# A new order of operations, wider output products and 1 KB weight packets in a DeltaNet and soft-MoE kernel

## The chip, the cores and the metric

The kernel runs on one core of a Trainium2 chip. A core has five engines that work side by side: TensorE (PE in the profile, with its weight loads as PEld), VectorE (DVE), ScalarE (ACT), GpSimd (POOL) and SyncE (SP, which here only issues DMAs). Data moves between main memory and the on-chip memory SBUF by 16 DMA engines; TensorE writes its results to PSUM, a small memory of eight banks, from which VectorE or ScalarE copies them out. DMAs are issued by SP, ACT and POOL. The metric is the time of one execution in microseconds; the median of several executions is compared.

## The reference

All data are float32. The first block is a DeltaNet recurrence over 768 positions, for 4 batches of 8 heads of width 48:

```
state = 0
for t in range(768):
    kt, vt, bt = k_n[:, :, t], v[:, :, t], beta[:, :, t]      # k_n: k over its norm
    y[t]  = q[t] . state
    state = state + bt * outer(kt, vt - state . kt)
```

Its output, as 3072 tokens of width 384, goes into a soft mixture of 8 experts with 4 slots each (32 slots):

```
logits     = x @ phi                           # 3072 x 32
slot_input = softmax(logits, over tokens).T @ x
for each expert e:                             # w1: 384 x 1024, w2: 1024 x 384
    slot_out[e] = relu(slot_input[e] @ w1[e]) @ w2[e]
out        = softmax(logits, over slots) @ slot_out
```

The experts' weights are 12.6 MB each for w1 and w2, 25.2 MB together, and are read once.

## The kernel before

**The recurrence.** It is worked in 12 chunks (called steps, n) of 64 positions, for all 32 pairs of batch and head at once, two chunks to a group g. Loads of k and v (L410) come as five DMAs for each half of the partitions, loads of q (L421) as one. For each chunk the kernel transposes k and q on TensorE (L473), forms their inner products (L504) and copies them out under masks on ACT and DVE. For each group it inverts a triangular matrix (`invert`, from L550): a chain of 15 columns, each a multiplication and a subtraction that the helper at L277 issues on DVE or on POOL, then `join` (from L641) with products on TensorE (L716, L761). Then `step` (from L803) multiplies the state with k (L821), the joined inverse with the rest (L840) together with the late part of the previous chunk's output (L782), updates the state (L867) and multiplies it with q (L791). `route` (from L894, transposes at L902) and `pair` (from L910; logits at L920, transposes at L945, L962 and L982, slot sums at L953) bring each finished group into the soft mixture.

**The experts.** The tokens' maxima are merged and the slot inputs formed (L1054 to L1069). `first` multiplies them with w1 in two batches of four experts (L1090, 24 matmuls for each half of the 1024 columns), clamps (L1099) and transposes (L1106). The second layer is worked in two halves of 192 output columns (h): 128 matmuls with w2 (L1123), a sum over experts (ACT at L1128, TensorE at L1129, DVE at L1130), and then the output products (`comb`, L1142) of the mixing weights with the slots. Each `comb` writes two PSUM banks with eight matmuls, one copy (through the helper at L281 on ACT or L283 on DVE) brings 768 columns to SBUF, and two puts with two DMAs each (L1150) write them out in runs of 768 B. In each half h there are six of these: three groups of tokens (g2) by two halves of rows (z).

**The order.** The code first describes 1164 operations with what they read and write, and then issues them in the sequence that a list written out in the file gives (ORDER, a list of the operations' numbers). Two further lists choose for each operation one of the engines it may run on (ALTS) and for each buffer its address in SBUF or its PSUM bank (PLACE). Semaphores between the engines follow from what each operation reads and writes; on one engine the instructions run in the list's sequence. The list was made ahead of time and the file holds only its result. The weights' loads (L1029 for w1, two DMAs of 256 KB for each of 24 tiles; L1040 for w2, two of 192 KB for each of 32 tiles) are operations of this list like all others, on SP or POOL, and each waits until the last work on its buffer's earlier contents is done.

Of the kernel before, what the change touches and what calls it, by code (L numbers as in the profile page):

```python
# [11 lines left out]
ALU = mybir.AluOpType  # L12
# [184 lines left out]
def kernel(  # L197
# [823 lines left out]
    for e in range(E):  # L1021
        for kk in range(NKT):
# [3 lines left out]
            def go(q, e=e, kk=kk, t=t):  # L1026
                s = moe_w1[e].rearrange("(p k) f -> p k f", k=NKT)
                for x in H2:
                    ENG[q].dma_start(out=A(t)[:, 512 * x:512 * x + 512], in_=s[:, kk, 512 * x:512 * x + 512])  # L1029
# [152 lines left out]
```

## Time and profile before

| | us |
|---|---|
| median of three runs | 296.75 (294.59 to 299.53) |
| the profiled execution | 296.42 |
| its span, first to last instruction | 294.7 |
| TensorE busy, matmuls | 228.9 (78%) |
| VectorE busy | 197.6 (67%) |
| ScalarE busy | 145.2 (49%) |
| GpSimd busy | 140.2 (48%) |

The profile is of one execution. Its span is divided into what each engine did; its chain follows the work that ended last back to the start, and names at each step what released it. "Issue" in the chain, or as the reason of a wait, is time in which an engine waited for nothing that the profile shows. A row of a timeline gives the start, the length, the engine and line, what was done, how many instructions were merged into the row, and in brackets how long the engine had been idle before and what ended that. A row of waits gives the engine and line, what it waited for, the total, the number of times and the longest. A row on the instructions of a line gives the least, the median and the greatest duration in ns. A small q behind an engine's name (SPq) marks its sequencer, which issues the DMAs.

By time the trace falls into four parts: the start, up to the first products at 7.9 us; the recurrence, with the mixture's logits inside it, up to about 248 us; the two expert layers, L1090 from 249.6 and L1123 from 262.5; and the output, whose first DMA is issued at 271.8 us.

### The profile page before, as it was taken

Reading aid. Unit: us, or ns where it says so; the run is one execution under the profiler, and the core shown is the slowest. Engines: PE = TensorE matmul, PEld = TensorE weight load, DVE = VectorE, ACT = ScalarE, POOL = GpSimd, SP = SyncE. Lnnn points to the kernel's source line nnn. Section 1 sums busy time; section 2 is a strip of 40 time slices with the busy share of each in tenths; the row PEclk is TensorE's granted clock in tenths of the full one; section 3 lists DMA queues with packets and bytes.
Section 4 is the critical chain, followed back from the end, with each engine's and each line's share of the span. In section 5 each row is a group of like instructions: output and inputs, shape, how many; then the busy total and the mean of one; then the engine's idle time right before and its main releaser. Section 6 shows DMA issues by size and latency. Waiting matters only on the chain.

```text
span 294.7 us, 14440 instructions
## 1 busy us (share of the span) xinstructions
PE 228.9 (78%) x6252; PEld 186.2 (63%) x6252; DVE 197.6 (67%) x504; ACT 145.2 (49%) x325; POOL 140.2 (48%) x225
## 2 busy tenths in 40 slices
PE   0784778982988897798979877787866988999950
PEld 0663677872887786686868775766654864366640
DVE  3468979989866689777699889883773667213130
ACT  1253487774828466668736768562311532230321
POOL 8997569454493364226762545641640320200460
PEclk9997599999579999999899999999997999999985
DMA  8979642453431361336545407785696599990887
GB/s 147 162 155 166 111 79 56 97 107 56 87 56 34 73 118 33 62 54 136 116 94 118 153 4 232 215 190 177 200 349 218 178 349 375 349 364 13 213 226 206
DMA packets 81519, 45.13 MB, mean 153 GB/s; under 512 B 63520, under 2 KB 74704, under 8 KB 81456
## 3 DMA queue, kind: packets, MB, share of 16 engines
q1 hardware_dynamic: 72704, 30.28, 42.3%
q0 software_dynamic: 5232, 12.56, 15.0%
q10 hardware_dynamic: 3520, 1.38, 2.0%
q8 instruction: 49, 0.80, 1.1%
q14 instruction: 14, 0.11, 0.1%
HBM read 39.47 MB, written 4.72 MB: 150 GB/s over the span
## 4 chain that ended last, share of the span: by engine, by line
PE 27%; DVE 12%; issue 8%; SPq 4%; ACT 4%; POOL 2%; DMA 1%; DVEq 0%; POOLq 0%; ACTq 0%
SPq L1150 4%; DVE sb L277 4%; PE pb L1090 4%; PE pb L716 3%; PE pb L821 3%; ACT sb L281 2%; PE pb L1123 2%; PE pb L782 2%; PE pb L902 2%; PE pb L791 2%; POOL sb L277 2%; PE pb L504 2%; PE pb L867 1%; PE pb L920 1%; PE pb L953 1%
## 5 line engine op out<-in xcount | busy, mean ns | idle before, releaser
L281 ACT ACTIVATE sb<-pb 128x512 f32<-128x512 f32 (+5 forms) x144 | 76.0, 559 | 91.2 <-PE pb L473 22.9
L277 POOL TENSOR_TENSOR sb<-sb 128x256 f32<-128x256 f32 (+10 forms) x89 | 64.7, 735 | 66.8 <-DVE sb L277 33.5
L277 DVE TENSOR_TENSOR sb<-sb 128x126 f32<-128x126 f32 (+10 forms) x153 | 52.9, 347 | 11.2 <-POOL sb L277 6.7
L283 DVE COPY sb<-pb 128x512 f32<-128x512 f32 (+5 forms) x43 | 26.2, 617 | 27.3 <-PE pb L473 5.9
L473 PE MATMUL pb<-sb 128*128 128x128 f32 x192 | 32.7, 318 | 15.0 <-DMA sb<-in_q_dram 9.6
L473 PEld LDWEIGHTS pb<-sb 128*128 128x128 f32 x192 | 24.7, 161 | 19.4 <-issue 11.7
L716 PE MATMUL pb<-sb 64*64 64x32 f32 x1152 | 27.3, 231 | 11.9 <-DVE sb L277 4.7
L716 PEld LDWEIGHTS pb<-sb 64*64 64x64 f32 x1152 | 25.0, 147 | 15.2 <-issue 7.3
L504 PE MATMUL pb<-sb 64*64 64x128 f32 x768 | 28.2, 287 | 5.8 <-ACT sb L281 4.2
L840 PE MATMUL pb<-sb 64*64 64x48 f32 x768 | 26.2, 220 | 3.9 <-DVE sb L770 1.9
L840 PEld LDWEIGHTS pb<-sb 64*64 64x64 f32 x768 | 24.2, 135 | 6.6 <-DVE sb L770 2.5
L504 PEld LDWEIGHTS pb<-sb 64*64 64x64 f32 x768 | 22.7, 140 | 9.0 <-ACT sb L281 5.4
L782 PE MATMUL pb<-sb 64*64 64x48 f32 x768 | 26.0, 220 | 2.3 <-issue 2.3
L782 PEld LDWEIGHTS pb<-sb 64*64 64x64 f32 x768 | 24.1, 135 | 2.7 <-issue 2.5
L1040 POOL DMA_DIRECT2D sb<-in_moe_w_dram x18 | 9.7, 543 | 32.9 <-PE pb L953 16.1
L821 PE MATMUL pb<-sb 128*64 128x96 f32 x352 | 19.2, 260 | 3.2 <-ACT sb L281 1.6
L791 PE MATMUL pb<-sb 128*64 128x96 f32 x352 | 18.9, 261 | 1.9 <-ACT sb L513 0.8
L412 POOL DMA_DIRECT2D sb<-in_k_dram x35 | 19.7, 570 | 0.7 <-DVE sb L341 0.7
L821 PEld LDWEIGHTS pb<-sb 128*64 128x64 f32 x352 | 16.8, 145 | 4.9 <-ACT sb L281 2.2
L1150 POOL DMA_DIRECT2D out_dram<-sb x14 | 8.4, 607 | 23.8 <-DVE sb L283 18.5
L513 ACT ACTIVATE sb<-pb,sb 128x128 f32<-128x128 f32 x48 | 16.9, 368 | 4.9 <-PE pb L504 4.7
L791 PEld LDWEIGHTS pb<-sb 128*64 128x64 f32 x352 | 16.4, 145 | 3.6 <-issue 1.5
(142 smaller groups left out, 376.4 us busy)
## 6 DMA issues: line engine op xcount, KB each, us to landing
sb<-in_moe_w_dram SPq DMA_DIRECT2D x46, 192.0 KB, 5.5
sb<-in_moe_w_dram SPq DMA_DIRECT2D x32, 256.0 KB, 4.0
sb<-in_moe_w_dram POOLq DMA_DIRECT2D x16, 256.0 KB, 5.3
sb<-in_moe_w_dram POOLq DMA_DIRECT2D x18, 192.0 KB, 6.1
sb<-in_q_dram SPq DMA_DIRECT2D x14, 192.0 KB, 4.4
out_dram<-sb SPq DMA_DIRECT2D x24, 96.0 KB, 3.5
sb<-in_v_dram SPq DMA_DIRECT2D x22, 96.0 KB, 3.3
sb<-in_v_dram SPq DMA_DIRECT2D x88, 24.0 KB, 2.8
```

The lines of the kernel that those rows point to most:

```text
L277: ENG[e].tensor_tensor(*a, **kw)
L281: nc.scalar.activation(o, i, ACT.Copy)
L283: V.tensor_copy(o, i)
L412: ENG[e].dma_start(out=d()[p0:p0 + w, x], in_=s[t0:t0 + w, hs])
L473: nc.tensor.transpose(A(ps)[:, 0, P * j:P * j + P], A(src)[:, x:x + P], ident())
L504: mm(A(ps)[ha(r), c, P * j4:P * j4 + P].rearrange("p (a t) -> p a t", a=2), x[ha(c), j, r, 0], x[ha(c), j, r])
L716: mm(A(ps)[ha(b), x, 64 * j:64 * j + RW].rearrange("p (a t) -> p a t", t=w), st, m)
L782: mm(pv(pY)[ha(1 - r), j // 4, j % 4, c], A(at)[ha(r), 512 * c + 64 * j:512 * c + 64 * j + 64], hv(u)[ha(r), j, c], start=first and c == 0 ...
L791: mm(A(pY)[ha(1 - r), j // 4, 96 * (j % 4):96 * (j % 4) + 96], kqv(KQ[n])[:, j, r, 1], Sv(n)[:, j, r], start=j % 4 == 0)
L821: mm(A(pR)[ha(r), j // 4, 96 * (j % 4):96 * (j % 4) + 96], kqv(KQ[n])[:, j, r, 0], Sv(n)[:, j, r])
L840: mm(pv(pW)[ha(r), j // 4, j % 4, c], A(zs)[ha(r), 64 * (zj * c + z0 + j):64 * (zj * c + z0 + j) + 64], hv(R)[ha(r), j, c])
L1150: ENG[e].dma_start(out=o[y, b, z][:, 2 * g2:2 * g2 + 2, HD * h:HD * h + HD], in_=A(ob)[ha(y), Dm * b:Dm * b + Dm].rearrange("p (x d) -> p ...
```

## The change

Three things change.

- All three lists are new. The new order comes from a search under 16 sets of disturbances. By the lists, TensorE's operations keep nearly their old sequence. Of the 24 tiles of w1, 22 are loaded by SP and 2 by POOL, where it was 16 and 8; of the 32 tiles of w2, SP has 23 and POOL 9, as before, though not the same ones. Among the elementwise operations of the recurrence, 12 more of the inversions' multiplications and subtractions run on POOL than before.
- The loads of w1 keep their two DMAs for each tile, but each now gathers two runs of 256 columns (1 KB) for each partition where it had one of 512 (2 KB). The columns then lie in SBUF in another sequence; the clamp puts them back.
- An output product covers both halves of rows (z): 16 matmuls, alternating over the four groups of 32 rows, into four PSUM banks. For two of the three groups of tokens, one of the pairs of banks is the one that holds the state's update during the recurrence (`pS`). The copies and puts are as before, in another sequence and on other engines. The program has 1158 operations.

```
             def go(q, e=e, kk=kk, t=t):
                 s = moe_w1[e].rearrange("(p k) f -> p k f", k=NKT)
                 for x in H2:
-                    ENG[q].dma_start(out=A(t)[:, 512 * x:512 * x + 512], in_=s[:, kk, 512 * x:512 * x + 512])
+                    ENG[q].dma_start(out=A(t)[:, 512 * x:512 * x + 512].rearrange("p (a f) -> p a f", a=2),
+                                     in_=s[:, kk].rearrange("p (a b f) -> p b a f", a=2, b=2)[:, x])
...
             def relu(e, f=f, ph=ph):
-                o = A(hr)[:, f * HF:f * HF + HF]
+                o = A(hr).rearrange("p (a b f) -> p b a f", a=2, b=2)[:, f]
+                i = A(ph)[:, 0].rearrange("p (a f) -> p a f", a=2)
...
         for g2 in range(NG // 2):
-            for z in H2:
-                po, ob = pl.buf(2, psum=True), pl.buf(2 * Dm)
-
-                def comb(po=po, z=z, g2=g2, so=so):
-                    for x in H2:
+            po = [pS if z == g2 % 2 == 0 else pl.buf(2, psum=True) for z in H2]
+            obs = [pl.buf(2 * Dm) for _ in H2]
+
+            def comb(po=po, g2=g2, so=so):
+                for x in H2:
+                    for z in H2:
                         for b in H2:
                             p0 = 32 * (2 * z + b)
                             g = 2 * g2 + x
-                            mm(A(po)[:, b, HD * x:HD * x + HD], A(cT)[p0:p0 + 32, P * g:P * g + P], A(so)[p0:p0 + 32])
-                pl.op("PE", 0.72, comb, r=[(cT, 2 * g2), (cT, 2 * g2 + 1), so], w=[po], rec=8, hold=[ob], act=384)
+                            mm(A(po[z])[:, b, HD * x:HD * x + HD], A(cT)[p0:p0 + 32, P * g:P * g + P], A(so)[p0:p0 + 32])
+            pl.op("PE", 0.8, comb, r=[(cT, 2 * g2), (cT, 2 * g2 + 1), so], w=po, rec=16, hold=obs, act=768)
+            for z in H2:
+                ob = obs[z]
...
```

In the new list all twelve puts of the first half stand ahead of the first output product of the second half, and on ACT three of them stand ahead of the copy at L1128 for that half.

More of the change, by code (lines that the diff above doesn't have):

```diff
@@ new lines @@
+    "0010000000000001010000010000000010001000001111101000110000100110100211210000011022000010000000001000"
+    "0001000000000010000000000001011000001100000000001000010100000001000000000110011001001110000110000001"
+    "0010021201010001100200000000000000000001010001000000001000000000010000101000000000001000010100000001"
+    "0000000000100001010000010100000000000100000001010000000110010001000212010000001000010000100000000000"
+    "0000000000000000010000000000100000000000000000000000101100000110010000000100000010000011010000020011"
@@ L121 @@
+    "1110011111010000000000101010002020101001110020000000000000010000000000000000000010100000000100000000"
+    "0000000100100010000000000000110000000000001000000000000100000010000000000000100100001000000010000010"
+    "0000000000001000000000001000000000001010100001001000000101000000110100000000000000000000000101000000"
+    "0000001010100122121012101000000000000000110000001010121121"
 )
@@ L1094, in relu @@
             def relu(e, f=f, ph=ph):
[L1095 removed]
+                o = A(hr).rearrange("p (a b f) -> p b a f", a=2, b=2)[:, f]
+                i = A(ph)[:, 0].rearrange("p (a f) -> p a f", a=2)
                 if e == "DVE":
[L1097 removed]
+                    V.tensor_scalar(o, i, 0.0, XMSK(qq), op0=ALU.max, op1=ALU.mult)
                 else:
[L1099 removed]
+                    nc.scalar.activation(o, i, ACT.Relu, scale=XMSK(qq))
             pl.op([("ACT", 0.69), ("DVE", 0.75)], None, relu, r=[ph, cxm], w=[(hr, f)])
```

21 lines of the change are left out of this document (5 added, 16 removed), and 172 rows, old and new, of tables (ORDER, PLACE).

## The prediction

> **What bounds the kernel now.** I read the page's shares first, then the chain of work that ended last, then the waits of TensorE, then windows of the DMA traffic, and last the tail's timeline.
>
> ```profile
> span 294.7 us, 14440 instructions
> PE 228.9 (78%) x6252; PEld 186.2 (63%) x6252; DVE 197.6 (67%) x504; ACT 145.2 (49%) x325; POOL 140.2 (48%) x225
> ...
> q8 instruction: 49, 0.80, 1.1%
> ...
> PE 27%; DVE 12%; issue 8%; SPq 4%; ACT 4%; POOL 2%; DMA 1%; DVEq 0%; POOLq 0%; ACTq 0%
> ```
>
> TensorE has the most work, and no engine is full. The chain changes engines all through the recurrence; 8% of the span, some 23 us, is "issue", in which the engine on the chain waits for nothing that the profile shows. The row of queue q8 says what that may be: 49 packets of program code, 0.80 MB, which is 16 KB each. TensorE has 6252 matmuls and 6252 weight loads; 12504 / 49 = 255 instructions, or 64 B of code for each. So TensorE's code streams in through the DMA engines all the time, beside the weights. Its waits between 183 and 225 us:
>
> ```profile
> PE pb L920 <- issue: 4.1, 1, 4.1
> PE pb L782 <- issue: 2.3, 2, 1.2
> PE pb L716 <- issue: 1.9, 2, 1.1
> PE pb L902 <- ACT sb L281: 1.0, 1, 1.0
> PE pb L821 <- issue: 0.8, 1, 0.8
> PE pb L791 <- issue: 0.8, 1, 0.8
> ```
>
> With "issue" that is 9.9 us in seven stalls, each inside a group of matmuls that are alike and need nothing new. The longest cuts one product in two, with the DMA engines full:
>
> ```profile
> 219.01 0.77 PE pb L920 x18
> 219.79 4.13 issue
> 223.92 0.58 PE pb L920 x6
> ```
> ```profile
> 212.00:224.00 12.00, 6.70 (x253) 5.68 (x253) 6.28 (x13) 1.28 (x5) 3.41 (x7) 1.00 0.97 335
> 224.00:240.00 16.00, 15.58 (x406) 12.99 (x410) 10.57 (x30) 5.24 (x15) 3.18 (x6) 0.89 0.64 206
> 240.00:264.00 24.00, 21.85 (x235) 10.68 (x231) 9.56 (x40) 8.77 (x25) 3.20 (x6) 1.00 1.04 368
> ```
>
> The columns are the stretch, the busy time of PE, PEld, DVE, ACT and POOL, TensorE's clock, the share of the DMA engines, and GB/s. At 212 to 224 the DMA engines are 97% busy with weights and TensorE works 6.7 of 12 us; at 240 to 264 they are full again, and TensorE works nearly all the time. So the recurrence's end loses about 10 us to code that comes late, and the two expert layers are bound by TensorE with the weights only just in time. The tail is different:
>
> ```profile
> 271.79 20.12 SPq L1150 DMA_DIRECT2D out_dram<-sb  x24
> ```
> ```profile
> 278.84 13.07 SPq L1150 DMA_DIRECT2D out_dram<-sb  x16
> 282.67 5.78 ACTq L1150 DMA_DIRECT2D out_dram<-sb  x4
> 289.41 1.84 ACTq L1150 DMA_DIRECT2D out_dram<-sb  x2
> ```
> ```profile
> L1150 SPq DMA_DIRECT2D out_dram<-sb x24: 595/626/1495, 271.8 to 291.3; - x24
> L1150 POOL DMA_DIRECT2D out_dram<-sb x14: 602/602/641, 272.9 to 286.8; - x14
> L1150 ACTq DMA_DIRECT2D out_dram<-sb x10: 602/622/780, 272.9 to 290.6; - x10
> ```
>
> SP and ACT issue as if they were one queue: 16 + 6 issues in 13.07 us are 0.594 us each, what one alone takes at best (595 ns). All 34 of the tail fill 271.79 to 291.9: 20.1 / 34 = 0.592. POOL issues beside them. The issue of the output by SP and ACT is the tail's bound, not TensorE.
>
> **The output products.** Each half of the output columns now has three product operations of 16 matmuls in place of six of 8.
>
> ```profile
> 269.84 0.95 PE L1142 MATMUL pb<-sb 32*128 32x192 f32 x16
> ...
> 275.62 0.92 PE L1142 MATMUL pb<-sb 32*128 32x192 f32 x8
> ...
> 279.91 4.35 PE L1142 MATMUL pb<-sb 32*128 32x192 f32 x48 [0.51 <-DVE sb L1130]
> ```
>
> ```profile
> L1142 PE MATMUL pb<-sb 32*128 32x192 f32 x96 | 8.9, 341 | 0.8 <-DVE sb L1130 0.5 <-DVE sb L283 0.2
> ```
>
> Sixteen over all four row groups take 0.95 us (the first row is two old operations of different halves, back to back), 8 alone take 0.92. Six operations of 0.95 are 5.7 us against 8.9 now: 3.2 us less TensorE work, worth nothing where the queue is full. It would be worth up to 3.2 us if copies waited for products. What counts is the split of the 24 copies out, of two DMAs each: the new list gives SP and ACT 15 (30 DMAs) and POOL 9, against 17 (34) and 7. Full from the first to the last, the queue would take 30 x 0.592 = 17.8 us, 2.4 less. I do not expect it full: on ACT the sum of the second layer's last half stands behind three copies out, and the queue runs dry near 278. From there I count 20 issues from 279.0: 279.0 + 20 x 0.594 = 290.9, against 291.9 now. **-1.0 us**, ends -2.4 and +1.2 (if ACT's copies hold the second half's start by two issues more). POOL, with 18 x 0.60 = 10.8 us, has room. Of its section on issuing engines, the Trainium skill (DMA: Bandwidth & Descriptors, "Issuing engines are not separate DMA queues") says that issuing from several engines saves the sequencers' issue time; SP and ACT at 0.594 us together show no such saving here. By that rule the second half's issues would end with SP's twelve alone, about 2.3 us sooner than I count.
>
> **First-layer weights.** The loads keep their bytes but are read in 1 KB runs, two for each partition in place of one of 2 KB.
>
> ```profile
> L1029 SPq DMA_DIRECT2D sb<-in_moe_w_dram x32: 327/382/1363, 133.6 to 250.2; - x32
> L1029 POOL DMA_DIRECT2D sb<-in_moe_w_dram x16: 536/537/603, 160.5 to 236.0; - x16
> ```
> ```profile
> L1040 SPq DMA_DIRECT2D sb<-in_moe_w_dram x46: 327/335/1575, 213.5 to 262.3; - x46
> ```
>
> A plain issue costs SP 0.38 us; the nearest with two runs for each partition is the output's, 0.60. The list puts 44 of these 48 DMAs on SP and 4 on POOL (32 and 16 before): on SP 44 x 0.60 - 32 x 0.38 = +14 us over 110 us, behind which loads of v and of the second layer wait. SP is on the chain for L1150 alone; behind step 10's product it has 14 x 0.60 + 42 x 0.33 = 22 us of issues in 45 us. I take **0**; without that cover the issues on SP cost their own length, 0.2 us a DMA. POOL gets 12 x 0.54 = 6.5 us back. For the transfer itself the nearest rows are the tail's 768 B packets and the stretch at 240:
>
> ```profile
> 271.80:291.90 20.10, 11.90 (x162) 8.92 (x162) 4.98 (x6) 5.18 (x7) 8.43 (x14) 0.84 0.83 221
> ```
>
> 221 / 0.83 = 266 GB/s of a full set of engines, against 368 / 1.04 = 354. A 1 KB packet lies between: 0 to 33% dearer. That matters only where the engines are full; little of the first layer falls there. It goes into the next term.
>
> **The lists.** Both lists hold TensorE's products in nearly the same sequence, so its work does not move. What moves is the weights. Counting from the lists: between step 8's product of the joined inverse (operation 903) and step 10's (951) stand 6.9 MB of weights before, 4.4 MB after, 36% less; behind step 10's stand 14.5 MB before, 16.5 after. In the trace the stretch between these products is roughly 189 to 219 us, that of the stalls.
>
> *Code stalls.* Bounds: 0 (the DMAs may still be issued in a burst as soon as buffers come free) and -9.9. I take them down with the bytes, 36%: **-3.5 us**. The Trainium skill (DMA: Bandwidth & Descriptors, "Queues, rings and completion order") states that an engine goes round its queues by packets of typically 9 to 17 descriptors. By that rule, halved descriptors would halve the wait of code behind first-layer loads, an estimate of -5 us; but a stall of 4.13 us is longer than one such packet of each queue, so the trace bears the rule out only in part.
>
> *The bus.* 2.0 MB more in the last stretch are 2.0 / 0.368 = 5.4 us of full bus. The stretch 224 to 240 has room for (368 - 206) x 16 us = 2.6 MB. Ends 0 and +5.4; I take **+1.0**, near the room, for packets that cost more and room that isn't met.
>
> *VectorE and GpSimd.* Net 16 elementwise operations go from DVE to POOL.
>
> ```profile
> 129.89 0.29 DVE sb L277
> ...
> 130.32 0.43 POOL sb L277
> ```
>
> On the chain each costs 0.14 us more, +2.2 in all; if DVE's queue is what is late, each takes 0.29 off it, -4.6. The chain alternates between both; **0**, with both ends kept.
>
> *The start.* POOL now clears a 1056-column buffer (L558) and a pad ahead of the identity matrix and of its half of k; the first q is split over two queues.
>
> ```profile
> 0.81 1.44 ACTq L421 DMA_DIRECT2D sb<-in_q_dram  x2
> ...
> 5.80 0.97 POOL L558 MEMSET sb<- 128x1056 f32 x1
> ...
> 7.89 1.09 PE L473 MATMUL pb<-sb 128*128 128x128 f32 x4 [7.89 <-DMA sb<-in_q_dram]
> ...
> 10.68 3.53 PE L473 MATMUL pb<-sb 128*128 128x128 f32 x15 [1.30 <-DMA sb<-in_k_dram]
> ```
>
> The first transposes may come sooner, but the second batch waits for k, whose POOL half moves back by up to 0.97 + 0.30 = 1.3 us. Ends -1.3 and +1.3; **+0.5**. The clamp's two-part pattern reads and writes the same elements, and the output's use of the recurrence's PSUM banks waits for work over since step 10: 0 each.
>
> **Sum.** -1.0 - 3.5 + 1.0 + 0.5 = -3.0 on the profiled execution's 296.42 us (span 294.7 and 1.7 around it): 293.4. The median of the runs shown, 296.75, is 0.3 above that execution, so I predict 293.7.
>
> **Rivals.** *The stalls go almost wholly* (8 to 9.9 us of them, with the tail's 1 to 2.4): 285 to 290. For it speaks that nothing else on TensorE is late there by more than 1.0 us; against it, that loads bunch behind step 10 as well, and the full bus at 240 to 264, which would wait for the same bytes. Chance 0.2.
>
> *The bus becomes the bound of the second layer* (the slower side). If buffers come free no sooner than the list places the loads, the 2.0 MB fall behind 240, into a bus that is full, and the second layer waits for its last weights: +5.4, with up to 1.4 for dearer packets (a third of the 4.7 MB of first-layer loads that stand behind step 10's product: 4.2 us x 0.33), no stall removed, the tail's -1.0: 300 to 303, up to 305 if the start's 1.3 and POOL's 2.2 come on top. It decides once less than 2.0 of the 2.6 MB of room is met. Chance 0.25.
>
> *The change does not do what it says*: loads bunch as before, code stalls move elsewhere, the tail gains nothing: 295 to 298. Chance 0.15. The forecast itself, 291 to 296, has 0.4.
>
> **How the numbers follow.** The range, 287 to 303, cuts off the lower part of the first rival and the upper end of the second, about 2 in 10. About 2%, 5.9 us, is what a measurement of this kernel tells from no change (its three runs span 1.7%). Below 290.8 lies the first rival and little else, 0.2; above 302.7 the upper part of the second, 0.16; within, 0.64.
>
> **What would show it.** Right: "issue" waits of TensorE between steps 8 and 11 near 6 us instead of 9.9; no wait of the second layer's products for weights; SP and ACT issues of the output at 0.59 us over about 19 us; L1142 with 16 in 0.95 us throughout. Wrong: weight loads landing behind the second layer's first product, new "issue" stalls after 224 us, or a recurrence whose steps come at other times for reasons of the list that no single row shows; the last is what could most easily upset the sum.

## The result, and the profile after

| | us |
|---|---|
| kernel before, beside the changed kernel | 298.14 (294.59 to 301.26) |
| changed kernel | 307.97 (307.21 to 313.19) |
| changed kernel, once more, in a later set of runs | 306.89 (305.25 to 307.69); before there 297.64 |
| ratio | 1.039, 95% interval 1.027 to 1.050; the second time 1.030, 1.023 to 1.037 |

The change makes the kernel slower by 3 to 4%, 9 to 10 us, where I had forecast 3 us less. The profiled execution of the first set took 313.19 us, 5 us over the median; so the profile shown here is that of the second set (307.69 us, span 306.0), and the first is called "the first profile" where it is used. Ratios leave disturbed executions out, so for a kernel whose executions lie far apart the ratio can be well under that of the medians.

The page's shares, and its clock row (tenths of full speed in 40 slices):

```profile
span 306.0 us, 14470 instructions
PE 229.3 (75%) x6252; PEld 187.0 (61%) x6252; DVE 199.5 (65%) x493; ACT 149.2 (49%) x328; POOL 142.8 (47%) x230
...
PEclk9996699998596999899999979999997799999955
```

TensorE's busy time is that of before (228.9), but only as a sum: its output products take 2.4 us less, and the recurrence and the expert layers, with the same products, 2.8 us more. Most of the 11.3 us more of span is idle time. Windows of both kernels say where; the columns are the stretch, the busy time of PE, PEld, DVE, ACT and POOL, TensorE's granted clock, the DMA engines' share, and GB/s. The stretches end where the last matmul starts of step 0's product, step 3's product, step 7's state update, step 8's product, the merge of the maxima, the last product of the second layer, and the end. Before:

```profile
0.00:52.10 52.10, 33.39 (x634) 28.76 (x636) 37.65 (x122) 24.82 (x59) 41.84 (x75) 0.90 0.73 125
52.10:99.80 47.70, 39.04 (x1245) 34.57 (x1242) 37.13 (x89) 29.55 (x61) 24.12 (x40) 0.89 0.40 73
99.80:177.90 78.10, 67.00 (x2277) 57.98 (x2272) 65.17 (x145) 51.95 (x115) 38.75 (x52) 0.98 0.40 86
177.90:188.80 10.90, 8.22 (x337) 7.26 (x328) 9.46 (x28) 7.17 (x17) 5.09 (x11) 1.00 0.79 224
188.80:249.00 60.20, 46.92 (x1339) 36.87 (x1329) 37.98 (x101) 21.57 (x58) 19.86 (x32) 0.97 0.78 254
249.00:277.70 28.70, 28.27 (x416) 16.12 (x416) 7.04 (x20) 6.39 (x13) 4.59 (x8) 1.00 0.74 241
277.70:294.70 17.00, 6.02 (x66) 4.65 (x58) 3.20 (x4) 3.76 (x6) 5.96 (x10) 0.73 0.80 219
```

After, the second profile:

```profile
0.00:53.90 53.90, 34.54 (x640) 29.34 (x640) 40.22 (x125) 25.79 (x61) 40.79 (x72) 0.91 0.77 125
53.90:104.30 50.40, 40.10 (x1234) 35.48 (x1231) 38.97 (x87) 28.84 (x60) 23.48 (x38) 0.83 0.38 66
104.30:184.20 79.90, 67.23 (x2271) 58.38 (x2271) 62.62 (x137) 52.11 (x114) 37.07 (x53) 0.96 0.41 93
184.20:198.60 14.40, 9.69 (x378) 8.72 (x367) 10.89 (x27) 10.45 (x23) 7.36 (x17) 1.00 0.38 93
198.60:259.40 60.80, 45.74 (x1307) 36.24 (x1298) 33.54 (x91) 23.90 (x58) 22.25 (x31) 0.94 0.85 267
259.40:287.00 27.60, 27.35 (x423) 15.40 (x423) 9.13 (x24) 5.48 (x10) 4.73 (x8) 1.00 0.66 221
287.00:306.00 19.00, 4.62 (x58) 3.39 (x50) 4.16 (x5) 2.65 (x4) 7.17 (x12) 0.63 0.78 208
```

Length less busy time is TensorE's idle time; length times (1 - clock) is what the half clock can have cost there, if TensorE was busy.

| stretch | length, change | idle before, after | (1 - clock) x length before, after |
|---|---|---|---|
| to step 0's product | +1.8 | 18.7, 19.4 | 5.2, 4.9 |
| to step 3's product | +2.7 | 8.7, 10.3 | 5.2, 8.6 |
| to step 7's update | +1.8 | 11.1, 12.7 | 1.6, 3.2 |
| to step 8's product | +3.5 | 2.7, 4.7 | 0, 0 |
| to the merge | +0.6 | 13.3, 15.1 | 1.8, 3.6 |
| both expert layers | -1.1 | 0.4, 0.3 | 0, 0 |
| the tail | +2.0 | 11.0, 14.4 | 4.6, 7.0 |
| sum | +11.3 | 65.9, 76.7 | 18.4, 27.3 |

There is no one hole. Every stretch of the recurrence has 0.7 to 2.0 us more of idle time, the tail 3.4, and there is more half clock. By what ended it, the idle time ahead of the first product with w1 grew in one kind alone in this pair: "issue" from 11.0 to 19.4 us, all the rest together 43.5 and 42.7. Of the 19.4 us, 7.6 lie ahead of the end of step 7's update, where this profile of the kernel before has none; the other seven profiles with its early lists have 1.1 to 4.4 there, so part of that belongs to the execution. Between 183 and 240 us the "issue" waits are much the same, 11.7 us in four lines against 11.0, and TensorE also waits for ScalarE's copies:

```profile
PE pb L840 <- issue: 5.6, 2, 4.2
PE pb L821 <- ACT sb L281: 3.2, 3, 2.3
PE pb L791 <- issue: 2.9, 1, 2.9
PE pb L867 <- issue: 1.9, 2, 1.3
PE pb L791 <- ACT sb L281: 1.5, 1, 1.5
PE pb L716 <- DVE sb L283: 1.5, 2, 0.8
PE pb L821 <- issue: 1.3, 1, 1.3
```

Between step 7's update and step 8's product the timeline shows what the order changed. The new list has ScalarE widen group 4's joined inverse in two instructions (L739) behind the four state copies, and all that the join still has to do comes behind that, up to VectorE's last operation (L770), which releases step 8's product at 196.47. The product of the state with k (L821) waits 2.34 us for the state copies. Step 9's product with q (the second L791) goes ahead of step 8's product, but costs nothing here: it ends at 196.43, L770 at 196.42:

```profile
183.55 0.90 PE L867 MATMUL pb<-sb 64*48 64x48 f32 x64
...
187.24 2.49 ACT L739 ACTIVATE sb<-sb 128x1024 f32<-128x1024 f32 x2
...
187.26 1.54 PE L821 MATMUL pb<-sb 128*64 128x96 f32 x32 [2.34 <-ACT sb L281]
...
190.30 1.54 PE L791 MATMUL pb<-sb 128*64 128x96 f32 x32 [1.50 <-ACT sb L281]
...
194.89 1.54 PE L791 MATMUL pb<-sb 128*64 128x96 f32 x32
...
195.01 1.41 DVE L770 SCALAR_TENSOR_TENSOR sb<-pb,sb 128x512 f32<-128x512 f32 x2 [0.88 <-PE pb L716]
```

Before, one half was on each of ScalarE and VectorE, and both were done ahead of the update, which ended at 178.12, so that a product of the join (L761) ran while the state was copied:

```profile
174.11 1.27 ACT L739 ACTIVATE sb<-sb 128x1024 f32<-128x1024 f32 x1 [0.82 <-DVE sb L733]
...
175.41 0.75 DVE L741 TENSOR_SCALAR sb<-sb 128x1024 f32<-128x1024 f32 x1 [0.23 <-ACT sb L739]
...
177.93 1.57 PE L761 MATMUL pb<-sb 64*64 64x32 f32 x64
...
180.94 1.54 PE L821 MATMUL pb<-sb 128*64 128x96 f32 x32 [1.44 <-ACT sb L281]
```

The state copies are no later than they were: from the update's end to L821 it is 2.8 us in both. From L821 to the start of step 8's product it is 5.6 us before (186.52) and 9.2 us after (196.47); that is where this stretch got longer.

In the tail the timeline of the second profile has ScalarE's sequencer issue six DMAs while its copy of the second half's sum (L1130) waits; TensorE stands for 2.72 us:

```profile
282.26 20.09 SPq L1155 DMA_DIRECT2D out_dram<-sb  x18
...
284.62 4.91 ACTq L1155 DMA_DIRECT2D out_dram<-sb  x6
...
285.77 1.51 PE L1125 MATMUL pb<-sb 128*32 128x192 f32 x32
...
289.63 0.32 ACT L1130 COPY sb<-pb 128x192 f32<-128x192 f32 x1 [7.43 <-DMA out_dram<-sb]
...
290.00 0.59 PE L1131 MATMUL pb<-sb 128*128 128x192 f32 x2 [2.72 <-ACT sb L1130]
...
291.10 3.75 PE L1145 MATMUL pb<-sb 32*128 32x192 f32 x48 [0.51 <-DVE sb L1132]
```

### The profile page after: what moved, and what is told of

It reads as the page before. It is cut to its first block, busy times and chain, and to the rows that moved or that the text cites. A ratio compares the mean times of both kernels' runs of the same rounds, so it can differ in the third digit from the quotient of the medians.

```text
span 311.5 us, 14470 instructions
## 1 busy us (share of the span) xinstructions
PE 240.2 (77%) x6252; PEld 196.2 (63%) x6252; DVE 197.4 (63%) x493; ACT 149.6 (48%) x328; POOL 142.6 (46%) x230
## 4 chain that ended last, share of the span: by engine, by line
PE 49%; DVE 22%; issue 9%; ACT 8%; POOL 4%; DMA 2%; ACTq 2%; SPq 1%; POOLq 0%; DVEq 0%
PE pb L473 7%; PE pb L716 6%; PE pb L840 6%; DVE sb L277 5%; PE pb L504 4%; PE pb L1091 4%; PE pb L791 4%; ACT sb L281 3%; PE pb L821 3%; POOL sb L277 3%; PE pb L1125 3%; PE pb L867 3%; PE pb L902 2%; PE pb L782 2%; PE pb L1145 2%
## 5 line engine op out<-in xcount | busy, mean ns | idle before, releaser
L281 ACT ACTIVATE sb<-pb 128x512 f32<-128x512 f32 (+4 forms) x141 | 76.0, 570 | 83.6 <-PE pb L473 24.9
L277 POOL TENSOR_TENSOR sb<-sb 128x256 f32<-128x256 f32 (+8 forms) x104 | 71.9, 701 | 96.2 <-DVE sb L277 40.0
L277 DVE TENSOR_TENSOR sb<-sb 128x96 f32<-128x96 f32 (+10 forms) x140 | 46.6, 335 | 12.4 <-POOL sb L277 8.6
L283 DVE COPY sb<-pb 128x128 f32<-128x128 f32 (+5 forms) x46 | 25.9, 580 | 33.6 <-PE pb L867 8.7
L473 PE MATMUL pb<-sb 128*128 128x128 f32 x192 | 35.0, 334 | 13.6 <-DMA sb<-in_q_dram 5.3
L716 PE MATMUL pb<-sb 64*64 64x32 f32 x1152 | 29.3, 236 | 13.8 <-DVE sb L277 4.2
L716 PEld LDWEIGHTS pb<-sb 64*64 64x64 f32 x1152 | 26.9, 153 | 17.6 <-issue 8.5
L473 PEld LDWEIGHTS pb<-sb 128*128 128x128 f32 x192 | 26.7, 172 | 17.7 <-issue 8.2
L840 PE MATMUL pb<-sb 64*64 64x48 f32 x768 | 30.5, 238 | 8.5 <-DVE sb L770 4.2
L840 PEld LDWEIGHTS pb<-sb 64*64 64x64 f32 x768 | 28.2, 154 | 11.4 <-DVE sb L770 5.1
L782 PE MATMUL pb<-sb 64*64 64x48 f32 x768 | 29.1, 231 | 0.5 <-issue 0.5
L504 PEld LDWEIGHTS pb<-sb 64*64 64x64 f32 x768 | 24.6, 149 | 6.5 <-ACT sb L281 4.4
L782 PEld LDWEIGHTS pb<-sb 64*64 64x64 f32 x768 | 26.8, 146 | 0.8 <-issue 0.7
L791 PE MATMUL pb<-sb 128*64 128x96 f32 x352 | 19.6, 264 | 4.7 <-issue 3.0
L821 PE MATMUL pb<-sb 128*64 128x96 f32 x352 | 18.3, 252 | 6.4 <-ACT sb L281 3.5
L1155 POOL DMA_DIRECT2D out_dram<-sb x18 | 10.8, 607 | 24.7 <-DVE sb L283 19.9
L821 PEld LDWEIGHTS pb<-sb 128*64 128x64 f32 x352 | 16.0, 140 | 8.2 <-ACT sb L281 5.5
L791 PEld LDWEIGHTS pb<-sb 128*64 128x64 f32 x352 | 16.9, 147 | 6.5 <-issue 3.8
```

The source lines that it names most:

```text
L277: ENG[e].tensor_tensor(*a, **kw)
L281: nc.scalar.activation(o, i, ACT.Copy)
L283: V.tensor_copy(o, i)
L473: nc.tensor.transpose(A(ps)[:, 0, P * j:P * j + P], A(src)[:, x:x + P], ident())
L504: mm(A(ps)[ha(r), c, P * j4:P * j4 + P].rearrange("p (a t) -> p a t", a=2), x[ha(c), j, r, 0], x[ha(c), j, r])
L716: mm(A(ps)[ha(b), x, 64 * j:64 * j + RW].rearrange("p (a t) -> p a t", t=w), st, m)
```

## The experiments

They are told in the order in which they were run. "Old" and "new" are the lists of the kernel before and of the changed one. The kernel before ran beside them with a median of 298.96 in the first set, then 297.78, 298.26, 297.64 and 297.64.

### Which of the three parts

**The packets.** In the changed kernel the loads of w1 and the clamp are put back; in the kernel before they alone are changed.

```
-  ENG[q].dma_start(out=A(t)[:, 512 * x:512 * x + 512].rearrange("p (a f) -> p a f", a=2),
-                   in_=s[:, kk].rearrange("p (a b f) -> p b a f", a=2, b=2)[:, x])
+  ENG[q].dma_start(out=A(t)[:, 512 * x:512 * x + 512], in_=s[:, kk, 512 * x:512 * x + 512])
```

> The changed kernel with the first layer's weights in runs of 2 KB again and the clamp as it was; the lists and the wide output products stay. The time to be explained is some 10 us (298 to 308). Theory A (the new lists make the recurrence and the tail late, packets do nothing): 306 to 309, the same as the changed kernel, and TensorE's issue stalls between steps 8 and 11 stay near 9 to 10 us. Rival B (1 KB runs slow the loads, and with them the code that TensorE waits for): 299 to 302, with those stalls shorter.

> The kernel before with the first layer's weights in runs of 1 KB and the clamp to match; its lists and its output products stay. Theory A: within 1% of before (295 to 301), SP's issue of a first-layer load 0.6 us in place of 0.38, issue stalls of TensorE between 183 and 225 us still near 10 us. Rival B: 303 to 308.

Changed kernel with 2 KB runs: 312.2 (303.85 to 318.26), above both ranges and too scattered to tell the theories apart. Kernel before with 1 KB runs: 299.07, ratio 1.0017 (0.9974 to 1.0060), with 9.7 us of "issue" between 183 and 240 us against 11.0 in the kernel before. So with the old lists the packets cost nothing and gain nothing that can be told; rival B is out there.

**The tail.** Old lists up to the second layer's first product, then the new ones, with the new output products and 1 KB runs (the edit is to the three lists alone). And in the changed kernel, three puts of the first half go from ScalarE to SyncE:

```
   # ALTS, operations 1114, 1115, 1117 (put)
-  ACT
+  SP
```

> The old order, engines and addresses up to the second layer's first product; from there on the new ones with the wide output products (five tail buffers at other addresses); 1 KB runs throughout. Theory A: the tail alone costs 2 to 4 us, 299 to 302, and the second layer's first product starts within 2 us of before's 262.5. If the tail were all of it: 307. If the tail cost nothing (rival C): 297 to 299.

> The changed kernel with three copies out of the first output half issued by SP in place of ACT, those that stand ahead of the copy that starts the second half. Theory A: the second half's sum starts as soon as TensorE has its products, about 2.5 to 3 us sooner after the second layer's end; 304 to 306. Rival C (the tail is bound by the issue of SP and ACT as one queue, whoever issues): no change, 307 to 309.

Old head and new tail: 301.29 (ratio 1.0068, 1.0005 to 1.0130), 2.2 us over the same kernel with the old tail (299.07). Three puts moved in the changed kernel: 306.18, ratio 1.0273 (1.0186 to 1.0360), 1.8 us under the changed kernel's first median and 0.7 under its second. So the tail loses about 2 us and the recurrence about 7.

### Which part of the recurrence

New lists up to the second layer with the old tail; old lists up to step 7's product and then the new ones; new lists up to there and then the old ones with the old tail (all with 1 KB runs).

> New lists up to the second layer's first product, then the old tail (products of one pair of row groups each) and its old order; 1 KB runs. Theory A, the new lists make the recurrence late: about 2 us under the changed kernel's 308.0, so 304 to 307, and 5 to 8 us over the kernel before. Rival T, the tail with ScalarE's output issues makes most of the loss: 298 to 301. Rival K, the recurrence is late only because TensorE's granted clock is halved longer: by chance of the run, anywhere from 300 to 307, with the time following the granted clock.

> Old lists up to the steps before step 7's product (about 163 us into the old trace), then the new ones, with the new tail and 1 KB runs. Theory A in its narrow form, it is the order around step 8 that costs: 304 to 307, with step 7's state update to step 8's product at 13 to 16 us (before 8.6, changed 12.2 in the slow profile and 14.1 in the run with three output issues moved). Rival E, the early lists cost (order up to step 7, and the half clock that comes with it): 300 to 302, as the kernel with the old head and the new tail (301.3).

> New lists up to step 7's product, then the old ones with the old tail; 1 KB runs. Theory A (narrow): step 8's group inverse is joined by ScalarE and VectorE before the state copies again, so step 7's update to step 8's product is 8 to 10 us, and the time 299 to 302, of which 1 to 3 us are brought from the steps before. Rival E: 303 to 307.

Measured: 308.31 (304.11 to 314.08), 305.74 (300.27 to 305.83), 305.72 (303.79 to 307.44; ratio 1.0298, 1.0216 to 1.0379). The first misses its range of 304 to 307 by its median, with a ratio of 1.0283 (1.0175 to 1.0391). The narrow form of theory A, that step 8 alone costs, falls: the early part alone loses nearly as much (6.7 over the 299.07 of the old lists), the late part alone 4.5 (over the 301.29 with the old head), and together they do not lose their sum. The 4.5 is the less sure of the two: one of the late part's four executions took 300.27, the other three 305.70 to 305.83. Rival T falls too; rival E, the early lists, holds for its half.

**The join of step 8 put back.** In the changed kernel the operations 676 to 685 go where the old list had them, with 677 on VectorE, and two of their PSUM buffers go to other banks.

```
   # ORDER; 890 is step 7's update, 900 and 902 step 8's product with k and what follows it,
   # 901 its product with q
-  ... 675, 751, ... 890, ... 732, 900, 676, 677, 678, 733, 775, 901, 780, 902, 679, 682, ... 684, 933, ... 685
+  ... 675, 676, 677, 678, 751, ... 732, 679, 733, 890, ... 682, 900, 680, 683, 681, 775, 684, 780, 902, 685, 901, ... 933
   # PLACE; the last two numbers are the first banks of the join's last two products
-  ... 50432, 51456, 4, 4, 4, 4, ...
+  ... 50432, 51456, 4, 4, 6, 6, ...
```

> The changed kernel; alone the operations that join group 4's inverse for step 8 are put where the old list had them: the widening ahead of step 7's state update with one half on VectorE, the rest behind it, and step 8's query product behind the join. Theory A: step 7's state update to step 8's product falls from 12 to 14 us to 8.5 to 10.5, and the time by 3 to 6 us, to 302 to 305. Rival S, the copies of the blocks of groups 10 and 11 queued on ScalarE and the next inverse on VectorE hold the state copies and the join as long as before, or the gain is taken back by steps 9 to 11: 306 to 309. Rival K, the clock: the time falls no further than the granted clock rises, 305 to 309 at a clock of 0.88 to 0.905.

312.43 (306.39 to 318.24), ratio 1.0356 (1.0251 to 1.0461): no gain. The profiled execution shows why the edit alone could not tell: step 9's product with q (933) was still ahead of step 8's product, and the clock was halved for most of the stretch. The edit also made a wait of its own. Banks 6 and 7, to which it moved the join, are those that step 8's product with q (901) writes; in the kernel before and in the changed one the two use different banks. So this product had to wait, 2.27 us, until VectorE's last operation of the join (L770) had read them.

### Is it the clock?

In the first profile TensorE was busy for 20.78 of 21 us between 41 and 62 us, at half clock; in the kernel before, for 19.44 of 21 at the full one. First the first profile, then before:

```profile
41.00:62.00 21.00, 20.78 (x359) 19.37 (x356) 13.55 (x34) 9.58 (x23) 11.06 (x18) 0.51 0.30 57
```
```profile
41.00:62.00 21.00, 19.44 (x541) 17.38 (x538) 18.59 (x50) 17.14 (x42) 14.68 (x25) 1.00 0.41 84
```

Half stretches seemed to follow short spells of little TensorE work. So gaps of TensorE were filled with products that nothing reads: identity by identity, into a PSUM bank that is free at that time.

```
+WARM = {164: (6, 0), 170: (4, 0)}      # behind which operation: how many, which bank
...
+            for x in range(WARM[i][0] if i in WARM else 0):
+                self.warm(WARM[i][1])
...
+    pl.warm = lambda b: mm(pb[:, b, 0:P], A(cident), A(cident))
```

> The changed kernel and ten idle products of 128x128 (identity by identity, into a bank that holds nothing yet) in two gaps of TensorE that the changed trace has at 35.70 to 36.86 and 37.96 to 38.77 us: six behind the last transposes of blocks 2 and 3, four behind the score product after them. Theory H, TensorE's granted clock falls to a half behind stretches of little TensorE work (in ten traces the half clock at 41 us came with five of the six early new lists and with none of the four early old ones, and everywhere a half stretch follows 3.4 us of low use): no half stretch at 41 us, step 0's product ends at 51.5 to 53 (changed 57.6, before 52.1), and the time falls by 3 to 6 us, to 302 to 305. Rival P, the clock is cut for too much work, not too little: the half stretch stays or grows, 307 to 312. Rival A, the lists' waits alone make the loss: 306 to 309 whatever the clock.

> The kernel before and 61 idle products of the same kind in its early gaps (18.9, 20.5, 21.8, 24.2, 27.7, 32.4 and 37.6 us) and 22 of these behind step 1's state update, where TensorE waits 4.73 us for VectorE. Theory H: the half stretches at 26.1 and 73.8 us (10.2 us each) get shorter or go; 2 to 7 us off the kernel before, 291 to 296. Rival P: longer half stretches, 299 to 304. Rival A: the clock is not on the path, 297 to 300.

> The changed kernel and 62 idle products in its early gaps (17.4, 21.7, 26.2, 30.6, 35.7, 38.0 us) and behind step 1's state update (75.7 to 79.9 us). Theory H: no half stretch at 41 and 79 us, step 3's product at 99 to 102 us (changed 110.2, before 99.8); 300 to 304, and what stays over the kernel before is the order around steps 8 to 11 and the tail (4 to 6 us). Rival P: 308 to 315. Rival A: 306 to 309.

Measured: 308.09 (304.38 to 312.32); 297.20, ratio 0.9921 (0.9874 to 0.9968); 307.23, ratio 1.0317 (1.0247 to 1.0387). The first has no half stretch at 41 us, as theory H has it, but not theory H's time. The gap of 4.73 us behind step 1's update shows the mechanism best. Windows of the kernel before, around the gap and behind it, and then those of the same kernel with idle products:

```profile
68.00:74.00 6.00, 1.27 (x94) 1.18 (x91) 5.79 (x10) 2.02 (x5) 1.57 (x2) 0.99 0.37 65
74.00:84.00 10.00, 9.75 (x179) 8.89 (x176) 7.53 (x17) 7.26 (x14) 6.05 (x7) 0.50 0.50 90
```
```profile
68.00:74.00 6.00, 5.79 (x131) 5.64 (x132) 5.79 (x7) 2.56 (x7) 2.38 (x2) 1.00 0.33 55
74.00:84.00 10.00, 8.58 (x273) 7.42 (x272) 8.87 (x21) 8.05 (x16) 5.76 (x7) 1.00 0.48 83
```

With the gap filled, the clock behind it stays at 1.00 and 273 matmuls run in the stretch in place of 179. Of the profiles of this study, all 15 without idle products in that gap have a half stretch that begins between 72 and 81 us, and none of the 5 with them has one. The clock falls for too little work: rival P is out. But the time hardly follows. The kernel before gains 0.8%, the changed kernel with all its early gaps filled nothing that can be measured: its profile is level with that of before at step 3's product (100.58 against 99.80 us), and yet it ends 9.6 us later, at a mean granted clock of 0.943 against 0.938. Its stretch from step 7's update to step 8's product, by windows:

```profile
180.80:197.90 17.10, 12.42 (x366) 11.14 (x360) 11.67 (x30) 9.98 (x22) 6.24 (x15) 0.80 0.43 111
```

17.1 us against 10.9: 4.7 idle, and the clock at 0.80 besides. So the clock by itself is not the loss, and rival A, the waits of the order, holds for the larger part. (That the half stretch at 41 us needs the gaps at 35 to 39 us is not shown: the second profile of the changed kernel lacks it without any idle product.)

**The tail again**, with the old head: the three puts on SyncE.

> The old lists up to the second layer's first product with the new output products, 1 KB runs, and the three output issues of ScalarE's that stood ahead of its copy for the second half put on SyncE. With those issues on ScalarE it took 301.3, with the old output products 299.1. Theory W, the new tail loses because ScalarE issues DMAs (5.05 us for six) while the second half's sum waits for its copy: 298 to 300. Rival C, the two queues issue as one (18 issues at 0.59 us on SyncE and ScalarE together), so moving them between the two changes nothing: 301 to 302. Rival O, the wide products themselves cost: 301 to 302 too, but with no wait of TensorE for that copy in the trace.

298.77 (296.30 to 301.85), ratio 1.0033 (0.9979 to 1.0087), 2.5 us less by the medians than with the puts on ScalarE (296.76 to 303.89) and level with the old tail. The two spreads overlap, so the trace decides. In its timeline the copy starts 0.07 us behind the last products where it started 2.35 us behind them in the second profile, and TensorE waits 0.44 us for it in place of 2.72:

```profile
276.81 1.51 PE L1125 MATMUL pb<-sb 128*32 128x192 f32 x32
...
278.39 0.32 ACT L1130 COPY sb<-pb 128x192 f32<-128x192 f32 x1 [5.20 <-PE pb L1125]
...
278.76 0.59 PE L1131 MATMUL pb<-sb 128*128 128x192 f32 x2 [0.44 <-ACT sb L1130]
```

Theory W holds: the wait, not the number of issues and not the wide products.

### Mending the places together

The changed kernel with step 8 mended in full (the join as above, and step 9's product 933 behind step 8's product 903); the same with the three puts on SyncE and 62 idle products; the old head with the mended tail and 31 idle products; and the changed kernel once more.

```
-  ... 804, 705, 933, 1013, ... 811, 903, 830, ...
+  ... 804, 705, 1013, ... 811, 903, 933, 830, ...
```

> As the kernel with the mended join of group 4 (312.4, at a clock of 0.84 to 0.90), and step 9's query product for block 8, which the new list has ahead of step 8's product, put behind it. By the account of TensorE's path, length is work plus idle time plus half of the time busy at the half clock: the stretch from step 7's state update to step 8's product has 9.7 of work and 5.0 idle in the changed trace, 8.2 and 2.7 before; so 10.5 to 12.5 us when mended, without a half stretch in it (changed 14.7). Theory Q, that place makes the late part: 302 to 306. Rival F, a floor behind it (code and weights loading until 233 to 239 us) takes the gain back: 306 to 310. The half clock at 41 us is free to come, so fast runs are the ones to compare.

> The changed kernel with all three mends: step 8's order as above, three output issues on SyncE instead of ScalarE, 62 idle products in the early gaps. Theory Q: 307.2 with the idle products alone, less 4 to 6 for step 8, less 2 for the tail: 299 to 302. Rival F: 304 to 307.

> The old lists up to the second layer's first product, the new output products with the three issues on SyncE, 1 KB runs, and 31 idle products in two gaps (nine behind the last transposes of blocks 2 and 3, 22 behind step 1's state update). Theory H: no half stretch at 73 us, 1.5 to 3 us under the same kernel without idle products (298.8): 295.5 to 297.5, under both kernels. Rival: the gain of the idle products in the kernel before (ratio 0.992) came from the other gaps, and nothing is left: 298 to 300.

> The changed kernel, once more. If the half stretch at 41 us belongs to the early order (five of six early new lists had it), it is there again, with step 0's product at 56 to 59 us and 305 to 313; if it was a matter of the run, it is away in about half of the runs, with step 0's product at 52 to 54 us and 303 to 308.

Step 8 mended: 307.52 (301.98 to 311.90). All three mends: median 304.90 of ten, from 297.09 to 308.72; ratio 1.0064 (0.9988 to 1.0139). Both medians lie in rival F's ranges, not in theory Q's. Old head, mended tail and idle products: 297.76 (295.71 to 304.16, and one at 378.45), ratio 0.9987 (0.9942 to 1.0032), no gain over the same kernel without them (298.77) that could be told. The changed kernel again: 306.89, with the half stretch at 41 us gone and the time the same. Step 8's stretch, by windows, first with that place mended, then with all three mends:

```profile
183.60:198.40 14.80, 10.55 (x336) 9.77 (x324) 9.04 (x25) 7.84 (x21) 10.19 (x20) 0.77 0.37 93
```
```profile
185.40:200.80 15.40, 12.24 (x342) 11.43 (x331) 9.59 (x27) 7.90 (x21) 10.24 (x20) 0.56 0.38 93
```

Step 9's product has left it (336 and 342 matmuls against 378), but it is no shorter: the clock is now halved in it, 14.8 x 0.23 = 3.4 us and 15.4 x 0.44 = 6.8 us, of which a part fell on idle time. And the wait that the mend itself brings is there: in the four profiles with the mended join (the join alone, step 8 mended, all three mends, and the mended late half below) step 8's product with q stands 2.2 to 2.8 us behind L770, and in none of the other sixteen. In the first of the two:

```profile
192.01 1.40 DVE L770 SCALAR_TENSOR_TENSOR sb<-pb,sb 128x512 f32<-128x512 f32 x2
...
193.47 2.83 PE L791 MATMUL pb<-sb 128*64 128x96 f32 x32 [2.75 <-DVE sb L770]
```

The expectation of 10.5 to 12.5 us missed, but the old order of step 8 has not been tried in the new list without that wait. Nor is rival F, a floor behind the stretch, shown: the stretch itself got no shorter.

**Each half of the recurrence by itself.** New early lists with the old late ones, and idle products (305.72 without); old early lists with the new late ones, step 8 and the tail mended (305.74 without).

> New lists up to step 7's product, then the old ones with the old tail and 1 KB runs (305.7 without the following), and 62 idle products in the early gaps. Theory H, the early loss is the half clock: 298 to 301, step 3's product at 99 to 102 us (106.9 without). Rival A, the waits of the early order remain: 303 to 306, with the idle time of TensorE up to step 7 more than 3 us over that of before.

> Old lists up to the steps before step 7's product, then the new ones (305.7 without the following), with step 8's join and query product put where the old list has them and three output issues on SyncE. Theory Q, these two places make the late loss: 298 to 301, with step 7's state update to step 8's product at 10.5 to 12.5 us and no wait of TensorE for ScalarE's copy of the second half. Rival F, other waits of the late order take their place: 302 to 305.

The first: 304.61 (300.48 to 309.60), ratio 1.0116 (1.0026 to 1.0205); the clock of its early stretches is nearly full (1.00, 0.93 and 1.00), and still it stands 7 us over the old lists with idle products (297.2). Its step 7's update ends at 181.3 us against 176.3, and TensorE is idle for 34.7 us ahead of that against 29.2. So with the gaps filled some 5 us of the early loss are waits of the order, as rival A has it. Without idle products, or with ten, the traces look otherwise: up to the same point TensorE is idle for 38.1 to 40.1 us with the old early lists and 37.4 to 42.3 with the new ones, and it is the time at half clock that differs, 24 to 31 us against 27 to 61. So waits and half clock seem to stand in for each other.

One of the waits is that for the join's last operation on VectorE (L770) ahead of step 2's product. Waits of TensorE between 50 and 180 us, first a row of the kernel before, then two of the second profile; the last, "issue", has no counterpart in this profile of before, but has one in others with the old early lists:

```profile
PE pb L840 <- DVE sb L770: 1.7, 2, 1.1
```
```profile
PE pb L840 <- DVE sb L770: 3.7, 3, 2.7
...
PE pb L716 <- issue: 2.4, 3, 1.2
```

The second: 301.16 (299.57 to 304.39), ratio 1.0104 (1.0042 to 1.0167), by the medians 4.6 us less than without the mends and 2.4 over the old head with the same tail; the 300.27 among the four without the mends makes the 4.6 unsure. Some 2.5 of it would be the tail, by the runs above. The rest is not step 8: that stretch takes 14.5 us where 10.5 to 12.5 were expected.

The traces of all twenty profiles say most plainly that both halves of the lists cost, the late one less clearly. Step 7's update ends at 176.3 to 179.8 us in the eight with the old early lists and at 181.0 to 192.5 in the twelve with the new ones. From there to the first product with w1 it is 70.3 to 73.4 us in the eight with the old late lists and 72.6 to 78.0 in the twelve with the new ones.

**What stays open.** With all three mends the kernel runs at 297 in some executions and at 308 in others; those under 301 us have a granted clock of 0.94 to 0.96, those above 303 one of 0.90 to 0.95. Why the clock falls in the one and not in the other was not found, nor were the many waits of 0.5 to 1.5 us of the early order taken apart one by one. How the early loss divides into waits and half clock stays open, and so does what step 8's old order would gain in the new list.

## Why the prediction was wrong

**The unpriced term.** The step that failed is the first of "The lists": "Both lists hold TensorE's products in nearly the same sequence, so its work does not move. What moves is the weights." The sequence did stay nearly the same, but that TensorE's time therefore stays does not follow: the copies and the join's operations between the products moved on ScalarE and VectorE, and the products come later or run at half clock. The runs showed it in this term's place: new early lists alone cost 6.7 us, new late ones alone 4.5, some 7 of the 9 to 10 together, and in every trace with new early lists step 7's update is late. Step 8 is the one place of it that is taken apart: there the join stands behind the state copies, and the product comes 3.6 us later behind L821. In the pair shown, the idle time of the first five stretches went from 54.5 to 62.2 us, and their busy time from 194.6 to 197.3. I had named the order as what "could most easily upset the sum" and gave it no bounds; a comparison of the two lists on ScalarE around each join (what stands ahead of the widening, of the state copies, of the product with k) would have pointed to step 8 without any run.

**The clock.** The sum has no term for TensorE's granted clock, although the second of its windows had 0.89 in it. Over 74 runs of the kernel before, 0.01 less of mean granted clock goes with 1.5 us more, and over 25 runs of kernels with the new lists through the whole recurrence (the changed one, and those with 2 KB runs, moved puts, ten idle products or the old tail) likewise; at a clock of 0.92 the two lines give 298.2 and 304.1. The medians of the changed kernel's clock were near 0.90. So about a third of the loss goes with the clock and two thirds do not. That is a correlation: waits can lower the clock as well as the clock the time, and 0.92 is the upper edge of the clocks of the new lists.

**Output products, -1.0.** The TensorE term held: 0.93 us for 16 matmuls, and 3 x 0.93 + 3.75 = 6.5 us in all against 8.9. The queue's pace held roughly: 30 issues of SP and ACT in 20.4 us (282.3 to 302.7), 0.68 each with the gaps between them, where I took 0.59. The failed step is the wait that I had seen and undersized: "on ACT the sum of the second layer's last half stands behind three copies out, and the queue runs dry near 278". I counted it as issues of the queue, with +1.2 as its worst. It is TensorE that stands, for 2.7 to 3.0 us, with the clock halved behind it (0.63 in the tail). It cost 2.2 to 2.5 us in place of the gain of 1.0. Nor does the gain come without the wait: from the start of the second layer's last matmul to the end it is 17.2 and 17.4 us in two profiles with the puts on SyncE, and 17.0 before. The prediction's 2.3 us, for a second half that ends with SP's twelve issues, cannot be followed from its rows: twelve issues of 0.594 us end 4.8 us ahead of twenty.

**Code stalls, -3.5.** Failed: 11.7 us of "issue" between 183 and 240 us in the second profile and 9.1 in the first, against 11.0 before; the prediction's 9.9 leaves out the shorter rows of its view. That these waits are for code, which I had inferred, the traces bear out (see the last section). The failed step is "I take them down with the bytes". Fewer weights between steps 8 and 10 in the list did not mean less traffic there: the DMA engines were 85% busy between step 8's product and the merge, against 78%. By the rule of the Trainium skill that I had quoted (DMA: Bandwidth & Descriptors, "Queues, rings and completion order"), halved descriptors would have let code through sooner. 1 KB runs alone left these waits at 9.7 us and the time at a ratio of 1.0017, so no run here shows it.

**The bus, +1.0.** The rival that had the second layer wait for weights did not come: both layers together took 27.6 us, 1.1 less than before, with TensorE busy for 27.35 of them.

**Packets and issue, 0.** Right, for a better reason than I had: an issue of w1 on SyncE went from a median of 0.38 to 0.42 us, not to 0.60. The second profile:

```profile
L1029 SPq DMA_DIRECT2D sb<-in_moe_w_dram x44: 367/416/1390, 142.1 to 249.0; - x44
...
L1029 POOL DMA_DIRECT2D sb<-in_moe_w_dram x4: 712/714/757, 218.4 to 255.5; - x4
```

**VectorE to GpSimd, 0, and the start, +0.5.** The first was not tried by itself. The start came out as +1.7 at step 0's product (53.85 against 52.11 us) in the second profile, a little over its upper end of 1.3.

## What to carry to other kernels

A list that keeps one engine's sequence can still move that engine's time: compare, for each product on the path, what the new list puts ahead of the copies it waits for on every other engine, and give that a term with bounds. Where an engine both computes and issues DMAs, look at which copy stands behind its issues, not only at the number of issues. Read TensorE's granted clock by stage before summing durations, since a wait of a few microseconds can be followed by work at half clock. And when a mend moves operations in such a list, look at the buffers they share with their new neighbours, or the mend brings a wait of its own.

## What the runs showed of the hardware

- Idle time of TensorE can bring half clock with it. The gap of 4.0 to 4.7 us behind step 1's update came with 7 to 10 us at half clock in all 15 profiles in which it was empty, and idle products took that stretch away in all 5 in which it was filled. The kernel's time hardly followed (ratio 0.9921 in the kernel before, no gain in the changed one). So long a gap is not needed: with step 8 mended, the clock fell at 186.5 us behind 3.4 us in which TensorE was busy for 1.96. The Trainium skill (TensorE: Matmul & The Clock Gate, "What's actually happening") says that an idle window of about 3.4 us halves the clock and one busy window restores it. The gap agrees with the first; against the second, the first profile has TensorE busy for 20.78 of 21 us and at half clock nearly throughout.
- TensorE's stalls without a visible cause go with program code here. Each "issue" wait of over 0.4 us after the first 10 us, 9 in the profile before and 12 in the second profile, ends 1.2 to 1.6 us behind the end of a 16 KB packet of queue q8, while the packet itself takes 0.9 to 1.7 us.
- Idle products in gaps of TensorE cost next to nothing: with 61 of them the kernel before took 297.2 us against 298.26, the only kernel of this study under both.
- Two runs for each partition in a load cost SyncE 0.03 to 0.04 us an issue and GpSimd 0.18 us (0.71 against 0.54).
